# Clustered attention with routed experts: products with v in groups of six key tiles, fourteen exp tiles, two small additions on ScalarE

## The chip, the cores and the metric

The kernel runs on one core of a Trainium2 chip. The metric is the device time of one execution in microseconds. The engines are named as in the profile: PE is TensorE's matrix products, PEld its loads of weights, DVE is VectorE, ACT is ScalarE, POOL is GpSimd, SP is SyncE, whose queue issues most DMAs. Each engine works through its own queue in order, and semaphores order the engines among each other.

## The reference

Two stages. The first is an attention over 4 batches x 8 heads x 768 rows of 64 elements in which a query sees only the keys of its own cluster; the second sends each row of the result to one of eight experts, or to none.

```python
q_assign = argmax(q_n @ c_n.T)            # 16 clusters a head; k likewise
mask = q_assign[:, :, :, None] == k_assign[:, :, None, :]
scores = where(mask, scale * (q @ k.T), -1e9)
attn = exp(scores - scores.max(-1))
attn = attn / (attn.sum(-1) + 1e-9)
x = (attn @ v), heads side by side         # 3072 rows x 512
...
do_compute = x @ w_skip > 0                # other rows pass unchanged
e_idx = argmax(xc @ w_gate)                # softmax over 8 experts gives gate_w
y = gate_w * (relu(xc @ w1[e]) @ w2[e])
out[do_compute] = xc + y
```

## The kernel before

The attention works on pairs of heads: 4 batches x 4 pairs are 16 pairs, numbered 0 to 15. A pair has 24 score steps (`score`, line 596): two halves of 384 queries (`hf`), six key tiles of 128 (`kt`), two heads (`a`). One step is two matrix products into one PSUM bank (lines 602 and 603), the exp on ScalarE into a tile of the ring `PT` (line 605), and an addition on GpSimd into the running sum of the half (lines 611 and 617). The scores stand transposed, with keys on the partitions, so the exp tiles are the right-hand side of the products with v.

Those products are `avs` (line 619). A call takes some key tiles of one half and issues, for each tile and head, one product into PSUM bank 7, the heads in the upper and the lower 64 partitions (128x64 tiles of the array, where the scores use 128x128). In the records each product shows as two. With `GROUP = 3`, a pair has four calls of six products, each set to wait for the last exp that it reads. The ring has `NPT = 12` tiles of 384 + 1 columns; exp number n goes to tile n mod 12.

Everything else of the stage runs between the steps of other pairs: for the next pair the row maxima (`smax`, line 562: one product, line 567, and one reduce on VectorE, line 569, 24 a pair) and the rows that carry them into the scores (`mneg`, `mrows`, lines 576 to 589); for the pair after that the products with the centroids (`sims`), the choice of the cluster (`assign` and `first_max`, five VectorE operations, lines 492 to 505), the split into a rounded part on ScalarE and a rest on VectorE (`split_hi` line 419, `split_lo` line 429) and the mask rows (`masks`); for the pair before, the sums (`sums` line 664, `recip` line 681), and the scaled output (`xout`: transposes, line 727, and six scaled copies on ScalarE, line 749). After every fourth pair the routing of a batch (`route_gates`, `route_slots`) is spread over the next pairs in small VectorE operations, among them lines 495, 912, 915 and 987.

The order of all this is written out by hand. `PLAN` gives each piece a due time in score steps, relative to its own pair; `FIRST` replaces some for the first pairs; `steps` puts all pieces of all pairs into one heap and emits them by due time. A piece that is a generator gives a number and comes back that many steps later. So one program order results, and each engine keeps to its part of it. The calls of `avs` come 1.6 steps behind their last tile: at 7.6, 13.6, 19.6 and 25.6 (which is 1.6 of the next pair). At 7.5 to 7.68 of a pair stand also `recip`, `xout`, `split_hi` and the last three operations of `assign`; at 19.65 to 19.7 a `split_lo`, the copies of `mrows` and operations of the routing.

Seven PSUM banks serve all but `avs`: `take` draws the bank that was given back first, and `give` puts it back behind the others, in program order.

`early_lists` gathers, near the end of pair 14, the first rows that an expert gets, and computes their gates in `slot_gates` (lines 1199 to 1204) from three columns. `group_hidden` and `group_result` serve rows beyond an expert's 256 places.

Of the kernel before, what the change touches and what calls it, by code (L numbers as in the profile page):

```python
# [13 lines left out]
F32 = mybir.dt.float32  # L14
# [4 lines left out]
AF = mybir.ActivationFunctionType  # L19
# [4 lines left out]
P = 128  # L24
H, S, D, NCL = 8, 768, 64, 16
HP = H // 2
HALF = S // 2
NB = HALF // P
KT = S // P
# [7 lines left out]
E, DM, FF = 8, H * D, 1024  # L37
KD, KF = DM // P, FF // P
CAP = 256
CT = CAP // P  # L40
OT = 64
# [22 lines left out]
    1: {  # L64
        "sims": -42.2, "hi": (-42.4, -42.3), "lo": (-40.1, -40.0), "copies": (-20.9, -20.8, -20.7), "load_v": -14.0,
        "assign": (-36.83, 12.93, 0.2, 0.2, 0.2, 0.2), "masks": (-21.6, 0.1), "smax": (-16.3, 0.95, -0.1),
        "mneg": (-5.3, 5.9), "mrows": ((-4.5, 0.2, 0.05), (6.4, 0.1, 0.05)),
    },
    2: {
        "load": -62.0, "load_v": -37.0, "hi": (-34.25, -28.3), "lo": (-28.35, -22.35), "copies": (-23.3, -23.2, -22.2),  # L70
        "assign": (-34.6, 0.25, 0.02, 6.0, 0.02, 0.02), "masks": (-26.0, 0.12), "smax": (-17.6, 0.97, 0.0), "mneg": (-6.4, 5.2),
    },
}

GROUP = 3


class Kernel:
# [6 lines left out]
    def run(self):  # L85
        tc = self.tc
        with ExitStack() as ctx:
            self.const = ctx.enter_context(tc.tile_pool(name="const", bufs=1))
            self.raw = ctx.enter_context(tc.tile_pool(name="rawp", bufs=RING))
            self.halves = {}  # L90

            self.both = ctx.enter_context(tc.tile_pool(name="both", bufs=1))
            self.D = self.both.tile([P, 66 * 256], F32R, name="D")
            self.NPT = 12
            self.PT = self.const.tile([P, self.NPT, HALF + 1], F32, name="PT")
            with ExitStack() as actx:
                self.attention(actx)
            with ExitStack() as mctx:
                self.experts(mctx)
# [146 lines left out]
    def buffers(self):  # L246

        D, both, last = self.D, self.both, self.nbatch * HP - 1
        assert last % 2 == 1 and last % 3 == 0
        part = lambda at, n, w: [D[:, at + w * j:at + w * (j + 1)] for j in range(n)]  # L250
        ops = [part(at, 4, S) for at in (13824, 0, 3072)]
        self.QM, self.KB = [o[:2] for o in ops], [o[2:] for o in ops]
        self.HI = part(6144, 2, S)
        self.QC = [part(at, 4, S) for at in (7680, 10752)]
        raw = both.tile([P, 2, 2, S], F32, name="raw", tag="raw")
        self.RAW = [raw[:, n] for n in range(2)]
        vt = both.tile([P, 2, KT, P], F32, name="vt", tag="vt")
        self.VT = [self.fix.tile([P, KT, P], F32, name="vt0"), vt[:, 0], vt[:, 1]]
        self.OT = [self.fix.tile([P, S], F32, name=f"oT{n}") for n in range(5)]

        w = part(0, 3, 1024) + [None] * 3 + [D[:, 6144:7168], D[:, 3072:4096]]
        w += part(4096, 2, 1024) + [D[:, 7168:8192], None] + part(8192, 2, 1024) + part(10752, 2, 1024)
        self.W = {"w1h": w[:4], "w1l": w[4:8], "w2h": w[8:12], "w2l": w[12:]}
        self.HT = [u.rearrange("p (f t) -> p f t", t=P) for u in part(13824, 2, 1024)]
        self.X1 = [u.rearrange("p (k t) -> p k t", t=P) for u in part(15872, 2, DM)]
        t = self.PT.rearrange("p n q -> p (n q)")
        self.HS, self.YE, self.XG0 = t[:, :FF], t[:, FF:FF + DM], t[:, FF + DM:FF + 2 * DM]
        self.XO = t[:OT, FF + 2 * DM:FF + 3 * DM]

    def keep_busy(self, n, w=4):  # L270

# [53 lines left out]
    def tasks(self, i):  # L325

        p, last = {**PLAN, **FIRST.get(i, {})}, i == self.npair - 1
        r = [(s, lambda s=s: self.score(i, s)) for s in range(NS)]
        add = lambda t, f, *a: r.append((t, lambda: f(i, *a)))
        if i:  # L330
            add(p["load"], self.load)
        add(p["load_v"], self.load_v)
        if i in (1, 2):
            add(-15.0 - i * NS, self.zero_rows)
        add(p["sims"], self.sims)
        add(p["assign"][0], self.assign, *p["assign"][1:])
        if i:
            for t in range(2):
                add(p["hi"][t], self.split_hi, t)
                add(p["lo"][t], self.split_lo, t)  # L340
            add(p["copies"][0], self.copies_hi)
            for t in range(2):
                add(p["copies"][1 + t], self.copies_lo, t)
            add(p["masks"][0], self.masks, *p["masks"][1:])
        else:
            for n in range(4):
                add(p["hi"][n], self.hi_first, n % 2, n // 2)
                add(p["lo"][n], self.lo_first, n % 2, n // 2)
            add(p["masks"], self.masks_first)
        t0, dt, gap, dt2 = (*p["smax"], p["smax"][1])[:4]  # L350
        for n in range(24):
            add(t0 + dt * n if n < 12 else t0 + 12 * dt + gap + dt2 * (n - 12), self.smax, n)
        for hf in range(2):
            add(p["mneg"][hf], self.mneg, hf)
            add(p["mrows"][hf][0], self.mrows, hf, *p["mrows"][hf][1:])
            for g in range(0, KT, GROUP):
                add(12 * hf + 2 * (g + GROUP) + p["av"], self.avs, hf, range(g, g + GROUP))
        if not last:
            add(p["sums"], self.sums, (0, 1))
            add(p["recip"], self.recip)  # L360
            for hf in range(2):
                add(p["xout"][2 if hf and i == self.npair - 2 else hf], self.xout, hf)
        if i == self.npair - HP - 1:
            for t, f in zip(p["early"], (self.early_lists, self.early_rows)):
                add(t, f)
        if last:
            for t, f, *a in self.ending(i):
                add(t, f, *a)
        elif i % HP == HP - 1:
            add(p["route"][0], self.route_a, i // HP)  # L370
            add(p["route"][1], self.route_gates, i // HP)
            add(p["route"][2], self.route_slots, i // HP)
        return r
# [284 lines left out]
    def sums(self, i, hfs):  # L658

        c, nc = self.st[i], self.nc  # L660
        sp = self.take("sums", [P, HALF])
        w = P // (2 * len(hfs))
        for n, (hf, a) in enumerate((hf, a) for hf in hfs for a in range(2)):
            nc.tensor.matmul(sp[n * w:(n + 1) * w, :], lhsT=self.ones[:, :w], rhs=c[f"acc{hf}{a}"],
                             start=True, stop=True)
        c["sr"] = self.small.tile([P, HALF], F32, name="sr")
        nc.scalar.activation(out=c["sr"], in_=sp, func=AF.Copy, bias=GUARD)
        self.give("sums")
        c["hfs"] = hfs
# [30 lines left out]
    def logits_last(self, i, hf, wait):  # L700
        nc = self.nc
        nc.tensor.matmul(self.last[64:96, :], lhsT=self.wg[:, HP - 1, :],
                         rhs=self.st[i]["oT"][:, hf * HALF:(hf + 1) * HALF], start=True, stop=True)
        yield wait
        self.sl = self.small.tile([P, HALF], F32, name="sr")
        if hf:
            nc.scalar.activation(out=self.sl[:96, :], in_=self.last[:96, :], func=AF.Identity, bias=self.guard[:96, :])
        else:
            nc.vector.tensor_scalar(out=self.sl[:96, :], in0=self.last[:96, :], scalar1=self.guard[:96, :], scalar2=None,
                                    op0=ALU.add)  # L710
        self.give("last")
# [487 lines left out]
    def slot_gates(self, acc, pool, rows, n, tag):  # L1199
        nc = self.nc  # L1200
        g = pool.tile([rows, n], F32, name=f"gate{tag}")
        nc.vector.tensor_tensor(out=g, in0=acc[:, 3, :], in1=acc[:, 4, :], op=ALU.add)
        nc.vector.tensor_tensor(out=g, in0=acc[:, 2, :], in1=g, op=ALU.add)
        return g
# [56 lines left out]
    def experts(self, ctx):  # L1261
# [79 lines left out]
        def group_hidden(w1):  # L1341
# [6 lines left out]
            for k in range(KD):  # L1348
                for c in range(2):
                    nc.tensor.matmul(ph[c * OT:(c + 1) * OT, :], lhsT=xt[:, k, :],  # L1350
                                     rhs=w1[k][:, c * FF // 2:(c + 1) * FF // 2],
                                     start=(k == 0), stop=(k == KD - 1), skip_group_check=True)
            hs = ot.tile([P, KF // 2, P], F32, name="ohs")
            nc.scalar.activation(out=hs.rearrange("p m f -> p (m f)"), in_=ph, func=AF.Relu)
            th = ps_y.tile([P, KF // 2, P], F32, name="py")
            for m in range(KF // 2):
                nc.tensor.transpose(out=th[:, m, :], in_=hs[:, m, :], identity=self.ident)
            ht = ot.tile([P, KF // 2, 2, OT], F32, name="oht2")
            nc.scalar.activation(out=ht.rearrange("p m c t -> p m (c t)"), in_=th, func=AF.Copy)
            return ht  # L1360

        def group_result(ht, w2, oid, og):
            py = ps_y.tile([P, DM // 2], F32, name="py")
            for f in range(KF):
                for c in range(2):
                    nc.tensor.matmul(py[c * OT:(c + 1) * OT, :], lhsT=ht[:, f % (KF // 2), f // (KF // 2), :],
                                     rhs=w2[f // 2][:, f % 2 * DM + c * DM // 2:f % 2 * DM + (c + 1) * DM // 2],
                                     start=(f == 0), stop=(f == KF - 1), skip_group_check=True)
            yo = ot.tile([OT, DM], F32, name="oyo")
            for c in range(2):  # L1370
                cs = slice(c * DM // 2, (c + 1) * DM // 2)
                nc.vector.scalar_tensor_tensor(out=yo[:, cs], in0=py[c * OT:(c + 1) * OT, :], scalar=og, in1=xo[:, cs],
# [118 lines left out]
```

## Time and profile before

| | |
|---|---|
| median of 3 runs | 668.26 us (664.48 to 669.05) |
| the profiled execution | 669.92 us |
| its span, first to last instruction | 668.1 us |
| mean granted TensorE clock | 0.989 |
| PE, DVE, ACT, POOL busy, share of the span | 96%, 76%, 63%, 53% |
| instructions | 12396 |

A row of the timeline gives the start, the duration, the engine, the line, the operation, what it writes and reads, the shapes, how many such instructions were merged, and in brackets the idle time of the engine before it with what ended it. A row of the windows gives the stretch, its length, then for PE, PEld, DVE, ACT and POOL the busy time and the count, then the granted clock, the share of the DMA engines and their rate. A row of a group gives the line, the engine, the shapes and count, then the busy time in us and the mean of one in ns.

### The profile page before, as it was taken

The numbers are of one execution on the slowest core, as the hardware profiler recorded it, in microseconds if no ns is written. First come the engines' busy times: TensorE is split into PE (matmuls) and PEld (weight loads), VectorE is DVE, ScalarE is ACT, GpSimd is POOL, SyncE is SP. The second block draws the span as 40 slices with busy tenths as digits, with TensorE's granted clock in tenths as the row PEclk, the third lists the DMA queues.
The fourth block names the chain that finished last, engine by engine and source line by source line (L and its number), as shares of the span: only waits on it lengthen the run. The fifth ranks groups of instructions, "written<-read, shape, count | busy, mean of one in ns | idle before, by whom it ended". The sixth has DMA issues, their size and how long they took to land.

```text
span 668.1 us, 12396 instructions
## 1 busy us (share of the span) xinstructions
PE 644.7 (96%) x3973; PEld 476.9 (71%) x3973; DVE 505.4 (76%) x1031; ACT 418.3 (63%) x933; POOL 357.3 (53%) x384
## 2 busy tenths in 40 slices
PE   7899999999999999999999998999899999999994
PEld 3666676677766767766767766556699899899793
DVE  7878786698998779997869899685769666765621
ACT  7567677777777777777777776543554544645420
POOL 8876776767767857767767688232032122121101
PEclk9999999999999999999999999799999999999998
DMA  7388557857775666466556541241476666764700
GB/s 213 112 195 230 141 163 205 209 164 189 213 217 139 167 170 161 120 170 173 153 134 167 144 117 59 61 146 64 140 259 219 217 225 234 226 208 166 263 10 34
DMA packets 54355, 110.18 MB, mean 165 GB/s; under 512 B 8615, under 2 KB 22823, under 8 KB 54288
## 3 DMA queue, kind: packets, MB, share of 16 engines
q1 hardware_dynamic: 51232, 101.92, 53.3%
q0 software_dynamic: 2656, 7.24, 3.2%
q8 instruction: 33, 0.54, 0.3%
q14 instruction: 34, 0.28, 0.1%
q10 hardware_dynamic: 400, 0.20, 0.1%
HBM read 61.00 MB, written 10.62 MB: 107 GB/s over the span
## 4 chain that ended last, share of the span: by engine, by line
PE 71%; DMA 10%; issue 9%; DVE 9%; POOL 0%; ACT 0%; POOLq 0%; DVEq 0%
PE ps L628 19%; PE ps L602 10%; PE ps L567 10%; PE ps L603 9%; DMA out<-yo,idw 6%; DVE M L569 3%; PE ps L727 2%; DMA xg<-out,idr 2%; PE ph L1028 2%; PE ph L1027 2%; PE ph L1026 2%; PE ps L584 2%; PE ps L478 1%; PE py L1028 1%; PE py L1026 1%
## 5 line engine op out<-in xcount | busy, mean ns | idle before, releaser
L617 POOL TENSOR_TENSOR acc<-acc,PT 128x384 f32<-128x384 f32 x246 | 240.6, 1006 | 56.8 <-ACT PT L605 56.6
L605 ACT ACTIVATE PT<-ps 128x384 f32<-128x384 f32 x384 | 184.5, 492 | 95.4 <-PE ps L603 78.4
L569 DVE TENSOR_REDUCE M<-ps 128x1 f32<-128x384 f32 x384 | 200.2, 554 | 46.1 <-PE ps L567 45.1
L628 PE MATMUL ps<-PT,vt 128*64 128x385 f32 x768 | 140.2, 500 | 0.0
L602 PE MATMUL ps<-D 98*128 98x384 f32 x384 | 135.1, 352 | 4.3 <-DVE M L569 3.8
L567 PE MATMUL ps<-D 96*128 96x384 f32 x384 | 134.9, 358 | 0.9 <-ACT D L547 0.7
L603 PE MATMUL ps<-D 128*128 128x384 f32 x384 | 130.4, 340 | 0.0
L602 PEld LDWEIGHTS ps<-D 98*128 98x128 f32 x384 | 73.1, 190 | 25.3 <-issue 19.1
L628 PEld LDWEIGHTS ps<-PT,vt 128*64 128x64 f32 x768 | 49.8, 137 | 57.8 <-issue 53.1
L611 POOL TENSOR_TENSOR acc<-PT 128x384 f32<-128x384 f32 x64 | 54.3, 870 | 68.3 <-ACT PT L605 36.6
L567 PEld LDWEIGHTS ps<-D 96*128 96x128 f32 x384 | 73.0, 191 | 21.3 <-issue 7.2
L1184 POOL DMA_INDIRECT out<-yo,idw x15 | 18.7, 1250 | 122.4 <-DVE yo L1060 111.0
L603 PEld LDWEIGHTS ps<-D 128*128 128x128 f32 x384 | 73.3, 191 | 0.0
L1309 DVE SCALAR_TENSOR_TENSOR hl<-ph,hh 128x256 fp32r<-128x256 f32 x56 | 23.7, 423 | 39.5 <-ACT hh L1308 39.5
L1308 ACT ACTIVATE hh<-ph 128x256 fp32r<-128x256 f32 x56 | 21.5, 383 | 46.8 <-PE ph L1028 45.8
L1280 ACT ACTIVATE D<-wraw 128x1024 fp32r<-128x1024 f32 (+1 forms) x45 | 43.9, 1001 | 7.6 <-PE py L1028 6.7
L1027 PE MATMUL ph<-x2h,D 128*128 128x256 f32 x168 | 47.5, 283 | 0.0
L1026 PE MATMUL ph<-x2l,D 128*128 128x256 f32 x168 | 47.4, 283 | 0.0
L1026 PE MATMUL py<-D,hh 128*128 128x512 f32 x112 | 45.1, 402 | 0.0
L749 ACT ACTIVATE x<-ps,rs 128x64 f32<-128x64 f32 x162 | 36.2, 322 | 10.2 <-DVE rs L681 9.1
L429 DVE TENSOR_TENSOR raw<-raw,D 128x768 fp32r<-128x768 f32 x28 | 39.2, 1401 | 0.0
L1281 DVE TENSOR_TENSOR D<-wraw,D 128x1024 fp32r<-128x1024 f32 (+1 forms) x29 | 34.3, 1185 | 6.2 <-ACT D L1280 5.2
(311 smaller groups left out, 1075.8 us busy)
## 6 DMA issues: line engine op xcount, KB each, us to landing
wraw<-w SPq DMA_DIRECT2D x72, 512.0 KB, 3.8
D<-D SPq DMA_DIRECT2D x124, 192.0 KB, 3.7
raw<-qk SPq DMA_DIRECT2D x16, 768.0 KB, 5.4
D<-raw SPq DMA_DIRECT2D x60, 192.0 KB, 4.1
vt<-v SPq DMA_DIRECT2D x16, 384.0 KB, 4.4
out<-x SPq DMA_DIRECT2D x31, 192.0 KB, 3.1
D<-mk SPq DMA_DIRECT2D x120, 24.0 KB, 1.9
out<-yo,idw POOLq DMA_INDIRECT x15, 3.7
```

What stands on the lines that cost most here:

```text
L429: eng.tensor_tensor(out=lo.bitcast(F32R), in0=lo, in1=c[f"hi{t}"].bitcast(F32), op=ALU.subtract)
L567: nc.tensor.matmul(sm, lhsT=c["qm"][a][0:96, j * P:(j + 1) * P], rhs=c["kb"][a][0:96, hf * HALF:(hf + 1) * HALF], start=True, stop=True)
L569: nc.vector.tensor_reduce(out=c["m"][:, j, a, hf:hf + 1], in_=sm, axis=AX.X, op=ALU.max)
L602: nc.tensor.matmul(ps, lhsT=c["kb"][a][0:98, ks], rhs=c["qm"][a][0:98, sl], start=True, stop=False)
L603: nc.tensor.matmul(ps, lhsT=c["kc"][a][:, ks], rhs=c["qc"][a][:, sl], start=False, stop=True)
L605: nc.scalar.activation(out=pt, in_=ps, func=AF.Exp, scale=D ** -0.5)
L611: nc.gpsimd.tensor_tensor(out=acc, in0=self.pt(i, s - 2)[:, :HALF], in1=pt, op=ALU.add)
L617: (nc.vector if dve else nc.gpsimd).tensor_tensor(out=acc, in0=acc, in1=pt, op=ALU.add)
L628: nc.tensor.matmul(av[a * D:(a + 1) * D, :], lhsT=c["vt"][:, kt, a * D:(a + 1) * D], rhs=self.pt(i, hf * 2 * KT + kt * 2 + a), start=(kt = ...
L1026: mm(ps, lhsT=ah, rhs=bl, start=first, stop=False)
L1027: mm(ps, lhsT=ah, rhs=bh, start=False, stop=False)
L1280: nc.scalar.activation(out=h[:, cs], in_=r[:, cs], func=AF.Copy)
```

## The change

`GROUP` becomes 6 for pairs 0 to 14, so that `avs` is called twice a pair, at 13.6 and 25.6, with twelve products a call; the last pair keeps groups of three. The ring gets 14 tiles. To make room, the tile `sr` has one buffer in place of two, and three tiles of the code for rows beyond 256 lie in the ring's memory. In `slot_gates` the one-column case, which is that of `early_lists`, uses two ScalarE activations with the second column as bias in place of two VectorE additions. Two entries of `FIRST` change: the rows of the maxima for pair 1 come 0.2 steps later, and the transposes of `assign` for pair 3 half a step later.

```diff
 FIRST, pair 1:
-        "mneg": (-5.3, 5.9), "mrows": ((-4.5, 0.2, 0.05), (6.4, 0.1, 0.05)),
+        "mneg": (-5.3, 5.9), "mrows": ((-4.3, 0.2, 0.05), (6.4, 0.1, 0.05)),
...
+    3: {"assign": (-41.95, 0.07, 0.02, 1.5, 0.02, 0.02)},
-GROUP = 3
+GROUP, LAST_GROUP = 6, 3
...
-            self.NPT = 12
+            self.NPT = 14
...
+        self.OHS, self.OHT, self.OYO = (t[:, FF + n * DM:FF + (n + 1) * DM] for n in (3, 4, 5))
...
-            for g in range(0, KT, GROUP):
-                add(12 * hf + 2 * (g + GROUP) + p["av"], self.avs, hf, range(g, g + GROUP))
+            group = LAST_GROUP if last else GROUP
+            for g in range(0, KT, group):
+                add(12 * hf + 2 * (g + group) + p["av"], self.avs, hf, range(g, g + group))
...
-        c["sr"] = self.small.tile([P, HALF], F32, name="sr")
+        c["sr"] = self.small.tile([P, HALF], F32, name="sr", bufs=1)
...
         g = pool.tile([rows, n], F32, name=f"gate{tag}")
+        if n == 1 and rows == P:
+            nc.scalar.activation(out=g, in_=acc[:, 3, :], func=AF.Identity, bias=acc[:, 4, :])
+            nc.scalar.activation(out=g, in_=acc[:, 2, :], func=AF.Identity, bias=g)
+            return g
         nc.vector.tensor_tensor(out=g, in0=acc[:, 3, :], in1=acc[:, 4, :], op=ALU.add)
         nc.vector.tensor_tensor(out=g, in0=acc[:, 2, :], in1=g, op=ALU.add)
...
-            hs = ot.tile([P, KF // 2, P], F32, name="ohs")
+            hs = self.OHS.rearrange("p (m f) -> p m f", f=P)
-            ht = ot.tile([P, KF // 2, 2, OT], F32, name="oht2")
+            ht = self.OHT.rearrange("p (m c t) -> p m c t", c=2, t=OT)
-            yo = ot.tile([OT, DM], F32, name="oyo")
+            yo = self.OYO[:OT, :]
```

More of the change, by code (lines that the diff above doesn't have):

```diff
@@ L704, in logits_last @@
         yield wait
-        self.sl = self.small.tile([P, HALF], F32, name="sr")
+        self.sl = self.small.tile([P, HALF], F32, name="sr", bufs=1)
         if hf:
```

## Prediction

> **What bounds the kernel now.** I read the page's busy shares first, then the windows, then the timeline around the groups of products with v.
>
> ```profile
> PE 644.7 (96%) x3973; PEld 476.9 (71%) x3973; DVE 505.4 (76%) x1031; ACT 418.3 (63%) x933; POOL 357.3 (53%) x384
> 27.40:429.60 402.20, 395.99 (x2444) 276.91 (x2443) 333.80 (x666) 293.84 (x707) 284.64 (x301) 0.99 0.60 162
> ```
>
> The second row is the window that holds all score tiles but the ends: TensorE is busy for 396.0 of 402.2 us, VectorE for 333.8. So the attention stage costs what TensorE's queue costs, and a change is worth the matrix time that it removes less the pauses that it makes. The 6.2 us that are missing are mostly one pause, shown below. The experts behind it (from 430 us) keep their work and only start earlier or later.
>
> **Part 1: two groups fewer a pair.** A pair issues its products with v (line 628) in four groups; pairs 0 to 14 get two. The number of products stays, so only what a group costs at its two ends can go.
>
> ```profile
> 258.83 0.49 PE L727 MATMUL ps<-ident,oT 128*128 128x128 f32 x3
> 259.25 2.16 PE L628 MATMUL ps<-PT,vt 128*64 128x385 f32 x12
> ...
> 261.62 0.34 PE L603 MATMUL ps<-D 128*128 128x384 f32 x1
> ...
> 265.30 0.49 PE L512 MATMUL ps<-ident,ss 128*128 128x128 f32 x3
> ...
> 265.80 0.34 PE L602 MATMUL ps<-D 98*128 98x384 f32 x1
> ...
> 410.67 0.14 PEld L628 LDWEIGHTS ps<-PT,vt 128*64 128x64 f32 x2 [0.18 <-issue]
> 410.99 0.14 PEld L628 LDWEIGHTS ps<-PT,vt 128*64 128x64 f32 x2 [0.18 <-issue]
> ```
>
> From three transposes to the second product behind them it takes 261.62 - 258.83 = 2.79 us with a group between, and 265.80 - 265.30 = 0.50 without: a group costs 2.29. Its twelve records are six steps of 0.32 to 0.325 (410.67 to 410.99), 1.94 us. So its ends cost **0.35 us**, and 15 pairs x 2 groups x 0.35 = **10.5 us** go.
>
> **Part 2: the early gates.** Two additions on one column move from VectorE to ScalarE.
>
> ```profile
> 409.95 7.17 POOL L617 TENSOR_TENSOR acc<-acc,PT 128x384 f32<-128x384 f32 x8
> 409.97 2.16 PE L628 MATMUL ps<-PT,vt 128*64 128x385 f32 x12
> 410.43 6.70 DVE L1202 TENSOR_TENSOR gatee<-slotacc 128x1 f32<-128x1 f32 x1
> ...
> 412.52 0.34 PE L567 MATMUL ps<-D 96*128 96x384 f32 x1
> ...
> 414.11 0.33 PE L567 MATMUL ps<-D 96*128 96x384 f32 x1
> 417.60 1.48 DVE L569 TENSOR_REDUCE M<-ps 128x1 f32<-128x384 f32 x3
> 418.20 0.69 PE L602 MATMUL ps<-D 98*128 98x384 f32 x1 [3.76 <-DVE M L569]
> ...
> 421.06 4.03 PE L628 MATMUL ps<-PT,vt 128*64 128x385 f32 x12
> ```
>
> The first addition took 6.70 us for one element a row; it ended when GpSimd's run of eight additions ended. The maxima (line 569) queue behind it on VectorE, TensorE stands 3.76 us, and then its clock is at half (part 4). Between these two groups lie 11.09 us, in pair 8 (253.44 to 259.25) 5.81: 5.28 us, and from 421.06 to 424.88 half of 3.82 more: **7.2 us** go. On ScalarE the two stand ahead of the row that frees a PSUM bank; at the nearest rows' 0.16 to 0.2 us each I charge 0.4. What is late next on VectorE is the two-input operation of line 987, right behind: at 201.77 (below) it took 0.87 beside GpSimd, which is small. The Trainium skill, "SBUF — State Buffer", section "Who interferes with whom", says that such a pair of engines excludes each other for one instruction. By that rule the addition should have waited 1.0 us, not 6.70, so the trace disagrees; by the rule the saving would be as here, for line 987 would wait once.
>
> **Part 3: what the removed groups covered.** The order of all other work stays. Seven PSUM banks go round in the order in which they are given back, two a score step (one score tile, one maximum tile). The fence above shows what that means: the maximum product at 412.52 was not reduced, and seven takes later, at 414.11 + 0.18 = 414.29, which is 1.77 us on, TensorE stopped; it went on 0.05 us after that reduce (417.60 + 0.55). So VectorE may be 1.77 us late between a product and the end of its reduce, no more. The two groups that go, after step 7.6 (call it A) and after 19.6 (B), stand exactly where VectorE and ScalarE have their long blocks. Even with the group in front, pair 0 shows a stop:
>
> ```profile
> 40.07 2.16 PE L628 MATMUL ps<-PT,vt 128*64 128x385 f32 x12
> 42.16 0.45 PE L567 MATMUL ps<-D 96*128 96x384 f32 x1
> ...
> 44.32 0.44 PE L567 MATMUL ps<-D 96*128 96x384 f32 x1
> ...
> 43.72 1.48 DVE L569 TENSOR_REDUCE M<-ps 128x1 f32<-128x384 f32 x3
> ```
>
> The product at 42.16 is reduced at 43.72; seven takes on, TensorE waits until 44.32.
>
> Place A, pair 8:
>
> ```profile
> 241.04 2.16 PE L628 MATMUL ps<-PT,vt 128*64 128x385 f32 x12
> ...
> 241.53 1.36 DVE L500 TENSOR_TENSOR eqc<-eqc,wts 128x384 f32<-128x384 f32 x1
> ...
> 243.50 0.56 DVE L505 TENSOR_TENSOR oh<-wts,mwc 128x384 bf16<-128x384 f32 x1
> 243.98 1.02 DVE L569 TENSOR_REDUCE M<-ps 128x1 f32<-128x384 f32 x2
> ...
> L500 DVE TENSOR_TENSOR eqc<-eqc,wts 128x384 f32<-128x384 f32 x14 | 12.0, 858 | 0.0
> ```
>
> Without the group the maximum product starts at 240.95, and the one that needs its bank is due at 242.72. Its reduce stands behind the reciprocals and lines 500, 503 and 505 of `assign`, none of which waits for the group (their inputs come from transposes ahead of it); it still starts at 243.98 and ends at 244.53, so TensorE goes on at 244.58: **1.86 us** late. (ScalarE's block, six scaled rows and a `split_hi`, ends at 243.7; its tile is needed 0.35 us after that point, so it adds nothing.) The block is shorter where line 500 meets no GpSimd: 1.36 here, mean (12.0 - 1.21)/13 = 0.83 in pairs 1 to 13, where the first of the 14, at 41.30 in pair 0, took 1.21. So 1.86 - 0.53 = 1.33 on the mean; 13 x 1.33 = 17.3, and for pair 14, which has no `assign` there but a scaling and a routing step, I take 1.0, an estimate from the short blocks: **18.3 us**. Behind the stopped score product stand the next score tiles, so ScalarE's exps, GpSimd's sums and the next maxima all wait for the same time; none of them is due before the next group, which is more than 1.5 us away.
>
> Place B, where a score tile comes first, so that the bank is due 2.12 us after the place:
>
> ```profile
> 173.54 2.16 PE L628 MATMUL ps<-PT,vt 128*64 128x385 f32 x12
> 173.79 1.55 DVE L429 TENSOR_TENSOR raw<-raw,D 128x768 fp32r<-128x768 f32 x1
> 176.14 0.94 DVE L915 TENSOR_TENSOR g<-g,vals 128x6 f32<-128x6 f32 x1
> 176.99 1.01 DVE L569 TENSOR_REDUCE M<-ps 128x1 f32<-128x384 f32 x2
> ...
> 253.44 2.16 PE L628 MATMUL ps<-PT,vt 128*64 128x385 f32 x12
> 255.33 0.64 DVE L495 TENSOR_TENSOR eqe<-L,mxe 128x48 f32<-128x48 f32 x1
> ...
> 201.77 0.87 DVE L987 TENSOR_TENSOR cc<-ohd,ecode 128x48 f32<-128x48 bf16 x1
> ...
> 225.69 2.16 PE L628 MATMUL ps<-PT,vt 128*64 128x385 f32 x12
> 225.94 1.61 DVE L429 TENSOR_TENSOR raw<-raw,D 128x768 fp32r<-128x768 f32 x1
> ```
>
> Pair 5: bank free at 176.99 + 0.60 = 177.59, due at 173.45 + 2.12 = 175.57, 2.0 late; so in 5, 9, 13. Pair 8, by its block's end at 255.97: 1.0; so in 4, 8, 12. In 6 and 10 the 0.87 of line 987 lies behind `split_lo`: 1.4. In 1, 2, 3, 7, 11, `split_lo` alone (225.94 to 227.55): 0.4. Sum 6.0 + 3.1 + 2.8 + 2.0 = 13.9. Pair 0 would be 2.6 late by the fence before, of which 1.1 comes back where it later waits for VectorE anyway (54.17, below): 1.5. **15.4 us.** At the two groups that grow to 4.0 us VectorE's and ScalarE's blocks were covered already, so nothing comes back there.
>
> **Part 4: the clock.**
>
> ```profile
> 418.05:424.88 6.83, 6.68 (x21) 3.67 (x21) 4.84 (x14) 2.87 (x4) 0.00 (x0) 0.50 0.20 47
> 479.49:482.90 3.41, 1.60 (x7) 0.84 (x6) 3.41 (x8) 3.41 (x7) 0.00 (x0) 1.00 0.47 150
> 482.90:486.30 3.40, 3.40 (x13) 2.80 (x12) 3.16 (x6) 1.99 (x5) 0.00 (x0) 0.50 0.93 331
> 52.83:56.24 3.41, 2.32 (x17) 1.83 (x17) 2.56 (x9) 1.87 (x5) 1.53 (x2) 1.00 0.95 243
> 54.17 0.55 PE L584 MATMUL ps<-ident,MX 128*128 128x128 f32 x3 [1.09 <-DVE MX L576]
> ```
>
> A 3.41 us stretch with TensorE busy for 1.60 was followed by 3.40 us at clock 0.50; one with 2.32 was not. Eight of the new stops (1.75 to 2.6 us: A where line 500 is long, in four pairs, and B in 0, 5, 9, 13) leave about 1.5 to 1.7 busy if they fall wholly into one stretch. I take two or three drops at 3.4/2 us: **+4 us**; bounds 0 and 8 x 1.7 = 14. The Trainium skill, "TensorE: Matmul & The Clock Gate", section "Part 1: The HAM clock gate", halves the clock after a whole idle window of some 3.4 us. By that rule these stops cost no clock, and the time would be 685; the row 479.49 speaks against it.
>
> **Small edits.** Two more exp tiles: tile n is overwritten by exp n + 14, whose readers stand ahead on TensorE and GpSimd; with 12, exp 12 and 13 would wait for the group. `sr` in one buffer: written once a pair, read 2.3 steps later. The overflow tiles in PT have no reader in flight. The two moved times of pairs 1 and 3 shift one set of transposes by one step: I take nothing, between 0.5 us either way (the length of such a set, 0.49 above). Without this cover the tiles would cost an exp's wait at each group.
>
> **Sum**: -10.5 - 7.2 + 0.4 + 18.3 + 15.4 + 4 = +20.4. The profiled execution took 669.92 us; 690.3. The median of the runs shown lies 1.66 below it: **689 us**.
>
> **Rivals.**
> (a) *Faster*: the stops don't come. It is decided at A: if the reduce behind `assign` ends within 1.77 us of its product, TensorE never stops. Then 669.9 - 10.5 - 6.8 - 1.7 = 651. For it speaks that TensorE runs full through the stage now; against it 40.07 to 44.32, and that the block's start hangs on nothing that moves. 0.12.
> (b) *The banks carry half*: blocks shorter or sooner by some 0.7 us each, as where GpSimd is idle: stops of 17 us cancel the gains, 668. 0.07.
> (c) *The gates don't bring what they say*: line 987 takes the place of the addition and starves as long: 689 + 7 = 696. Against: 0.87 at 201.77. 0.07.
> (d) *The clock drops at nearly every stop*, 1.1 us ones too: 24 x 1.7 = 41 in place of 4: 726; half of them, 706. The row 52.83 speaks against. 0.08.
> My forecast (stops as read, up to eight drops: 677 to 700): 0.66.
>
> **Numbers.** About 1% (6.7 us) is what a measurement of this kernel can tell from no change. Range 669 to 706: forecast and (c), the upper edge of (b) and the lower part of (d). Faster 0.12, same 0.07, slower 0.81.
>
> **What would show it.** Right: line 628 in 24-record groups of 4.0 us; in each of pairs 1 to 13 a TensorE pause of 1 to 2 us some 1.8 us behind the transposes of line 727 at A, put down to line 569; a shorter one after line 584 at B; GpSimd and ScalarE no busier; line 1202's early row gone from VectorE. Wrong: TensorE at full pace through A, or pauses put down to ScalarE or GpSimd. Should the exp of step 11 not be done at the longer group, a wait for line 605 would stand ahead of line 628.

## The result, and the profile after

The changed kernel takes **699.0 us** (median of 4 runs, 697.73 to 699.78) against 667.55 in the same runs of the kernel before: ratio 1.047, 95% interval 1.0428 to 1.0511. It is slower by 31 us; forecast were 689, range 669 to 706. The profiled execution took 699.78 us, 29.9 more than that of before.

The page of the changed kernel, busy shares and clock in 40 slices:

```profile
PE 653.7 (94%) x3973; PEld 482.0 (69%) x3973; DVE 493.1 (71%) x1029; ACT 407.8 (58%) x935; POOL 363.2 (52%) x384
PEclk9989999999989999999999999999999999999998
```

VectorE's and ScalarE's shares fell, GpSimd's hardly changed, and TensorE's went from 96% to 94% of a longer span: TensorE waits. For whom, says the view of waits (engine, line, releaser: us in total, times, longest), limited to TensorE:

```profile
PE ps L605 <- DVE M L572: 10.3, 12, 1.7
PE ps L528 <- DVE M L572: 2.9, 1, 2.9
PE ps L587 <- DVE MX L579: 2.9, 5, 1.2
PE ps L969 <- DVE M L572: 2.2, 2, 1.3
PE ps L570 <- ACT x L752: 2.2, 6, 0.6
```

Lines have moved by three: 605 is the score product that was 602, 570 the maximum product (567), 572 its reduce (569), 631 the product with v (628). Before, the first of these rows was one wait, the one behind the gates. Now the reduces hold TensorE at a dozen places by the first row alone. A wait is counted here only beyond the time in which the product before it is still drawn as busy, so the rows understate the stops; start to start is the better reading. Place A of pair 8, TensorE and VectorE in the timeline:

```profile
262.77 0.42 PE L570 MATMUL ps<-D 96*128 96x384 f32 x1
...
264.28 0.33 PE L606 MATMUL ps<-D 128*128 128x384 f32 x1
264.92 0.55 PE L817 MATMUL ps<-ident,gs 128*128 128x128 f32 x3 [0.31 <-ACT x L752]
266.50 0.55 PE L817 MATMUL ps<-ident,gs 128*128 128x128 f32 x3 [1.03 <-DVE M L572]
...
268.75 4.10 PE L631 MATMUL ps<-PT,vt 128*64 128x385 f32 x24
272.79 0.44 PE L570 MATMUL ps<-D 96*128 96x384 f32 x1
...
263.44 1.36 DVE L503 TENSOR_TENSOR eqc<-eqc,wts 128x384 f32<-128x384 f32 x1
264.83 0.55 DVE L506 TENSOR_REDUCE mwc<-eqc 128x24 f32<-128x384 f32 x1
265.42 0.56 DVE L508 TENSOR_TENSOR oh<-wts,mwc 128x384 bf16<-128x384 f32 x1
265.89 1.94 DVE L572 TENSOR_REDUCE M<-ps 128x1 f32<-128x384 f32 x4
```

The maximum product of 262.77 is reduced from 265.89 to 266.44, behind the same three operations as before, and 0.06 us later, at 266.50, the product that needs its bank starts. The 0.31 us before it, for ScalarE's scaled rows (line 752), cost nothing of their own: the wait for VectorE ends later. The long group then takes 4.04 us (268.75 to 272.79), the products of two groups with one pair of ends in place of two.

Place B of pair 5, and the clock in the windows (length, busy times and counts of PE, PEld, DVE, ACT, POOL, then the granted clock) around it:

```profile
189.23 0.44 PE L570 MATMUL ps<-D 96*128 96x384 f32 x1
191.34 0.44 PE L605 MATMUL ps<-D 98*128 98x384 f32 x1 [1.67 <-DVE M L572]
...
187.50 1.61 DVE L432 TENSOR_TENSOR raw<-raw,D 128x768 fp32r<-128x768 f32 x1
189.03 0.97 DVE L915 CAST vals<-g 128x6 bf16<-128x6 f32 x1
190.04 0.78 DVE L918 TENSOR_TENSOR g<-g,vals 128x6 f32<-128x6 f32 x1
190.74 1.94 DVE L572 TENSOR_REDUCE M<-ps 128x1 f32<-128x384 f32 x4
...
188.77:192.18 3.41, 1.74 (x9) 1.27 (x9) 3.38 (x7) 1.67 (x5) 3.41 (x4) 1.00 0.49 151
192.18:195.59 3.41, 3.41 (x14) 1.78 (x14) 3.38 (x8) 2.20 (x8) 2.16 (x3) 0.50 1.06 265
```

The stop, 2.11 us from start to start, left 1.74 us busy in a stretch of 3.41, and the next 3.41 us ran at half clock.

### The profile page after: what moved, and what is told of

It reads as the page before. It is cut to its first block, busy times and chain, and to the rows that moved or that the text cites. A ratio compares the mean times of both kernels' runs of the same rounds, so it can differ in the third digit from the quotient of the medians.

```text
span 698.0 us, 12396 instructions
## 1 busy us (share of the span) xinstructions
PE 653.7 (94%) x3973; PEld 482.0 (69%) x3973; DVE 493.1 (71%) x1029; ACT 407.8 (58%) x935; POOL 363.2 (52%) x384
## 4 chain that ended last, share of the span: by engine, by line
PE 57%; DVE 19%; DMA 11%; issue 9%; ACT 1%; SPq 1%; POOL 0%; POOLq 0%; DVEq 0%; ACTq 0%
PE ps L631 18%; DVE M L572 8%; PE ps L605 7%; DMA out<-yo,idw 6%; PE ps L570 6%; PE ps L606 6%; DVE raw L432 2%; DMA xg<-out,idr 2%; PE ps L481 2%; PE ph L1030 2%; PE ph L1029 2%; PE ph L1031 2%; PE ps L587 1%; PE ps L667 1%; DVE eqc L503 1%
## 5 line engine op out<-in xcount | busy, mean ns | idle before, releaser
L620 POOL TENSOR_TENSOR acc<-acc,PT 128x384 f32<-128x384 f32 x246 | 243.7, 1019 | 44.0 <-ACT PT L608 43.8
L572 DVE TENSOR_REDUCE M<-ps 128x1 f32<-128x384 f32 x384 | 195.4, 550 | 90.6 <-PE ps L570 90.1
L608 ACT ACTIVATE PT<-ps 128x384 f32<-128x384 f32 x384 | 175.6, 498 | 133.9 <-PE ps L606 99.5
L605 PE MATMUL ps<-D 98*128 98x384 f32 x384 | 139.9, 364 | 13.4 <-DVE M L572 10.3
L570 PE MATMUL ps<-D 96*128 96x384 f32 x384 | 138.5, 367 | 4.9 <-ACT x L752 2.2
L631 PE MATMUL ps<-PT,vt 128*64 128x385 f32 x768 | 136.5, 504 | 0.0
L606 PE MATMUL ps<-D 128*128 128x384 f32 x384 | 132.4, 345 | 0.0
L614 POOL TENSOR_TENSOR acc<-PT 128x384 f32<-128x384 f32 x64 | 55.7, 890 | 108.5 <-ACT PT L608 66.2
L631 PEld LDWEIGHTS ps<-PT,vt 128*64 128x64 f32 x768 | 53.5, 141 | 66.3 <-issue 63.8
L606 PEld LDWEIGHTS ps<-D 128*128 128x128 f32 x384 | 74.8, 195 | 0.0
```

Of the source, the lines that this page charges most:

```text
L570: nc.tensor.matmul(sm, lhsT=c["qm"][a][0:96, j * P:(j + 1) * P], rhs=c["kb"][a][0:96, hf * HALF:(hf + 1) * HALF], start=True, stop=True)
L572: nc.vector.tensor_reduce(out=c["m"][:, j, a, hf:hf + 1], in_=sm, axis=AX.X, op=ALU.max)
L605: nc.tensor.matmul(ps, lhsT=c["kb"][a][0:98, ks], rhs=c["qm"][a][0:98, sl], start=True, stop=False)
L606: nc.tensor.matmul(ps, lhsT=c["kc"][a][:, ks], rhs=c["qc"][a][:, sl], start=False, stop=True)
L608: nc.scalar.activation(out=pt, in_=ps, func=AF.Exp, scale=D ** -0.5)
L614: nc.gpsimd.tensor_tensor(out=acc, in0=self.pt(i, s - 2)[:, :HALF], in1=pt, op=ALU.add)
```

## Experiments

Theory: the two groups that went had covered VectorE's blocks at A and B, whose reduces free the PSUM banks; the stops let the clock fall. Rivals: the longer group, the 14 tiles or the new order cost by themselves; VectorE is short of time wherever its work stands. The ratios are to the kernel before in the same job (medians 668.2, 668.3 and 667.6 us).

**e1, the gates alone.** The kernel before with the `slot_gates` branch of the change.

> The kernel before with one edit: the two early additions go to ScalarE. My theory of the gates: the 3.76 us pause of TensorE and the half clock behind it go, 7.2 us less 0.4 for ScalarE, so 661 us against 667.6. Rival: the two-input operation of line 987, which moves into the place of the addition, is starved as long by GpSimd's run of eight; then 667.

Measured 667.01 us, ratio 0.9992 (0.9979 to 1.0005): the rival holds. VectorE in the timeline:

```profile
410.43 6.75 DVE L987 TENSOR_TENSOR cc<-ohd,ecode 128x48 f32<-128x48 bf16 x1
417.22 0.20 DVE L990 TENSOR_REDUCE c<-cc 128x6 f32<-128x48 f32 x1
417.34 1.48 DVE L569 TENSOR_REDUCE M<-ps 128x1 f32<-128x384 f32 x3
```

Line 987 took the addition's place and its 6.7 us. It was never a matter of one element.

**e2, the blocks of A moved.** Changed kernel with

```diff
-"assign": (-42.45, 0.07, 0.02, 2.0, 0.02, 0.02)    "masks": (-34.5, 0.12)   "xout": (31.52, ...)
+"assign": (-42.45, 0.07, 0.02, 8.05, 0.02, 0.02)   "masks": (-26.0, 0.12)   "xout": (37.5, ...)
 FIRST, pair 3:
-"assign": (-41.95, 0.07, 0.02, 1.5, 0.02, 0.02)
+"assign": (-41.95, 0.07, 0.02, 7.55, 0.02, 0.02)
```

`xout` of pair 14 keeps its times.

> The changed kernel, with the blocks at place A put beside the long group: the last three VectorE operations of assign go from step 7.64 to 13.69, the first half of xout from 7.52 to 13.5, and the mask rows, which need assign, to step 22. My theory (the removed groups had covered these blocks): the stops at A go. In the trace of the changed kernel steps 8 to 14 of pairs 1 to 14 are 23.5 us longer than before beyond the 1.94 us of the grown group, three half-clock stretches included, so 699 - 23 = 676. Rival 1 (the longer group, the 14 tiles or the order of the exps cost by themselves, wherever the blocks stand): 699. Rival 2 (VectorE as a whole is the bound of the new order): the time shows up at the next place, 690 or more.

675.22 us, ratio 1.0116 (1.0096 to 1.0136): 24 us off by due times alone, as forecast to 1 us. Rivals 1 and 2 fall for A.

**e3, the blocks of B moved.**

```diff
-"lo": (-34.35, -28.35), "copies": (-23.3, -23.2, -23.1)   GATES 43.67, 43.68 / 67.67, 67.68   SLOTS 91.67, 91.68
+"lo": (-34.35, -22.35), "copies": (-23.3, -23.2, -22.2)   GATES 49.64, 49.65 / 73.64, 73.65   SLOTS 97.64, 97.65
 FIRST, pair 2:
-"lo": (-28.35, -22.35), "copies": (-23.3, -23.2, -22.2), "assign": (..., 6.0, ...),  "masks": (-26.0, 0.12)
+"lo": (-22.36, -22.35), "copies": (-23.3, -22.3, -22.2), "assign": (..., 12.0, ...), "masks": (-22.0, 0.12)
```

> The changed kernel, with the blocks at place B put beside the long group: the second split_lo from step 19.65 to 25.65 with the copies behind it, the routing steps of 19.67 to 25.64, and in pair 0 the first split_lo and three operations of assign from 19.65 to 25.65. Theory: the stops at B go, 18 us in steps 20 to 24 of pairs 0 to 13 and some 6 us of half clock in the pairs behind them, so 699 - 24 = 675; 680 if the drops of the clock come from A as well. Rival 1: 699. Rival 2: 690 or more.

680.95 us, ratio 1.0213 (1.0191 to 1.0235): 18 off. Steps 20 to 24 of pairs 2 to 13 are now 0.2 us longer than before the change, where they were up to 2.0. Less than 24 came back for two reasons: pairs 6 and 10 still drop the clock behind A, and a stop in pair 1 is new, the next point.

**e4, both.**

> Both moves together. Theory: no stop of TensorE over 0.5 us is left between pair 1 and 14, and what remains is what parts 1 and 2 of the prediction gave: 667.6 - 10.5 - 6.8 = 650, with up to 4 us for blocks that no longer fit beside one group (VectorE has some 4 to 5 us of work at step 13.6, ScalarE 2.7): 650 to 655, faster than both kernels. Rival 1: near 699. Rival 2: 675 or more, since the same VectorE work is only pressed into fewer places.

664.79 us, ratio 0.9964 (0.9951 to 0.9977): a little ahead of before, yet 10 to 15 us short of what I expected. In pairs 2 to 14 TensorE is nowhere idle for more than 0.6 us. Of what is missing, 5 us (664.79 to 659.8, as e5 shows) stand at one place, of my own making:

```profile
48.78 0.33 PE L607 MATMUL ps<-D 128*128 128x384 f32 x1
52.60 0.50 PE L529 MATMUL ps<-ident_bf,oh 128*128 128x128 bf16 x3 [3.48 <-DVE oh L509]
```

The mask products of pair 2 waited for an `assign` that I had moved too late, with 6.8 us of half clock behind. Most of the rest is that a group that goes is worth less than its 0.35 us, as the pairs of e5 show.

**e5, that `assign` beside the first long group.** In `FIRST`, pair 2: `"assign": (-34.6, 0.25, 0.02, 0.02, 0.02, 0.02), "masks": (-26.0, 0.12)`.

> As both moves together, but the three operations of assign that pair 0 does for pair 2 go beside its first long group (step 13.7) and the mask rows stay at 22. My theory of the 12 us that the two moves still lacked: in pair 0 I had put that assign at 25.7 and the mask products behind it, where TensorE stood 3.5 us (48.78 to 52.60) and ran 6.83 us at half clock after it, 7 us in all. Then 664.8 - 7 = 658, ahead of both kernels by more than 1%. Rival (VectorE is short of time in pairs 0 and 1 in any order): the stop shows up at the next wait for VectorE, 663 to 665.

**659.8 us** (659.23 to 660.82), ratio 0.988 (0.9854 to 0.9906): ahead of both kernels, 2 us above what I expected. Place A of pair 8 now, TensorE and then VectorE:

```profile
242.99 0.49 PE L731 MATMUL ps<-ident,oT 128*128 128x128 f32 x3
243.41 4.10 PE L632 MATMUL ps<-PT,vt 128*64 128x385 f32 x24
247.44 0.44 PE L571 MATMUL ps<-D 96*128 96x384 f32 x1
...
243.75 1.57 DVE L433 TENSOR_TENSOR raw<-raw,D 128x768 fp32r<-128x768 f32 x1
245.25 0.94 DVE L875 TENSOR_REDUCE L<-lp 128x54 f32<-128x432 f32 x1
246.10 0.54 DVE L504 TENSOR_TENSOR eqc<-eqc,wts 128x384 f32<-128x384 f32 x1
247.27 0.56 DVE L509 TENSOR_TENSOR oh<-wts,mwc 128x384 bf16<-128x384 f32 x1
```

Four microseconds of VectorE stand beside the group. What the grouping is then worth is small: an ordinary pair is 0.25 us shorter than before the change, not 2 x 0.35 = 0.70; the rest goes into 0.2 us at B, where TensorE waits for a bank whose exp stands behind the rows of the maxima on ScalarE, and into mask products at a place of their own. The pause behind the early gates is gone here too; e8 below, which keeps groups of three and takes away that pause alone, reaches 661.12. So e5 is 1.3 us ahead of the best that was found without regrouping.

**e6, the stops filled.** Changed kernel with idle bf16 products ahead of the stops.

```diff
+            for t, n in ((10.85, na), (23.95, nb), (21.95, 0 if i else 13)):   # na 5 to 10, nb 0 to 8 by pair
+                if n: r.append((t, lambda n=n: self.keep_busy(n)))
```

> The changed kernel, with idle products (bf16, 128x512, results unused, into the bank of the products with v while it is free) put in TensorE's queue just ahead of its stops: 5 to 10 at A, 5 to 8 at the long stops of B, 13 ahead of the mask products of pair 0, each some 0.22 us. VectorE's order, and so the end of each stop, stays; only the idle time goes. Theory (half the clock's time is lost because TensorE idles in the stops): the half-clock stretches of pairs 0 to 14 (23.9 us in the changed kernel, 12 us lost) go, 699 - 12 + up to 3 for products that last beyond a stop: 687 to 690. Rival (the clock falls for another reason, or the stops are longer because of it): 699 or more.

690.48 us, ratio 1.0332 (1.0296 to 1.0368): half a microsecond above the upper end. From pair 1 on no half clock is left in the attention; the mean granted clock is 0.993 where the changed kernel has 0.978. The pairs are as long as those of the changed kernel less the 12 us of its drops, but for 2.6 us in all, where products last beyond a stop. So at least 8.5 us of the 31 were the clock, and idle time in the stops was its cause.

**e7, groups of three, all else of the change kept** (`GROUP, LAST_GROUP = 3, 3`).

> The changed kernel with groups of three in every pair, everything else of the change kept: 14 tiles, sr in one buffer, the gates on ScalarE, the two moved times. Theory (the grouping alone makes the kernel slower): as the kernel before with the gates alone, 667. Rival (the ring or the moved times cost): 670 or more.

668.79 us, ratio 1.0011 (0.9991 to 1.0032). The ring, `sr` and the moved times cost nothing that can be measured: the grouping alone made the kernel slower.

**e8, the early gather behind the gates**, in the kernel before:

```diff
-        yield 0.2
-        self.gather(self.xe[:, 0, :], rd, self.ntok - S)
         yield (91.66,)
         self.early = wr, self.slot_gates(acc, const, P, 1, "e")
+        yield (91.95,)
+        self.gather(self.xe[:, 0, :], rd, self.ntok - S)
```

> The kernel before, gates on VectorE as there, with the gather of the early rows issued after them (step 19.95 in place of 13.87). On ScalarE's account the gates brought nothing, since line 987 in their place took 6.75 us too. Theory: GpSimd is behind at that place because the gather held its queue for some 2.8 us, and a VectorE operation with two inputs waits as long as GpSimd's additions follow each other without a gap; without the gather in front the addition takes 1 us at most and the pause goes: 667.6 - 7 = 660.5. Rival (something in the operation itself, or in its place behind the maxima): again 6.7 us, 667.

661.12 us (661.0 to 661.33), ratio 0.9897 (0.9863 to 0.9931): the pause is gone, and this is the cheapest gain found. VectorE, then GpSimd:

```profile
410.37 0.59 DVE L1202 TENSOR_TENSOR gatee<-slotacc 128x1 f32<-128x1 f32 x1
411.00 0.79 DVE L1203 TENSOR_TENSOR gatee<-slotacc,gatee 128x1 f32<-128x1 f32 x1
...
409.12 3.65 POOL L617 TENSOR_TENSOR acc<-acc,PT 128x384 f32<-128x384 f32 x4
412.94 1.22 POOL L1179 DMA_INDIRECT xe<-out,idre  x1 [0.17 <-issue]
```

That the early gather's place decides is shown. That it does so through GpSimd's unbroken run is only argued: here too the additions follow each other closely, and VectorE got in at the first change-over.

**e9, the ring at 12 tiles**, on e5.

> As the best version so far (both moves, pair 2's assign early), with 12 exp tiles in place of 14. Exps 12 and 13 of a half then overwrite tiles 0 and 1, which the first four records of the long group read, so they wait until about 0.7 us into that group; ScalarE's scaled rows and split_hi stand behind them. Theory: the group lasts 4.0 us and ScalarE has some 3.6 us to do in it, so the wait stays covered: 660 to 662, and the two tiles are hardly needed. Rival (the prediction's sentence that the tiles would cost an exp's wait at each group, 27 places of about 0.5 us): 670 or more.

671.28 us, ratio 1.0059 (1.0036 to 1.0081), 11.5 over e5. My reasoning had the order the wrong way round: exps 12 and 13 stand ahead of the products in the program, so the exps don't wait for the products; the products wait for the exps, and the first key tile's products read the exps of the next half, so that the output is wrong. This run tells of the order and the time alone. All records of line 632, by who ended their engine's idle time (e5 has 4.0 us, 23 times, in this row):

```profile
  ACT PT L609: 9.6, 50
```

The long group becomes 4.41 us, 0.37 more. Fourteen tiles are what groups of six need, not a cover.

## Why the prediction was right, and where it was off

Sign, mechanism and places came out as read; the range held, with the forecast 10 us too low. By its terms, with steps compared from start to start between the traces of before and after:

- *Ends of groups, 0.35 us each*: the stretches that lost a group are 2.29 us shorter, those that grew 1.94 longer in pairs without a stop. As predicted.
- *A, 18.3 us*: steps 8 to 14 of pairs 1 to 14 are 23.5 us longer beyond the grown group; three drops of the clock among them (5.1) leave 18.4. That the sum agrees to 0.1 is partly luck. Pairs 4 and 12 lost 1.0 where I read 1.9, since line 503 took 0.53 us there and not 1.35. Pairs 6 and 10 lost 1.8 to 1.9 where I read 1.4, since line 964 of the routing took 1.21 and 1.07 us there and not 0.40.
- *B, 15.4 us*: steps 20 to 24 of pairs 0 to 13 add 18.05; less 0.9 that pair 1 regained and 1.3 of half clock, 15.8. Pair by pair 0.3, 0.3, 1.1, 2.0, 1.5, 0.2 for pairs 2 to 7, where 0.4, 0.4, 1.0, 2.0, 1.4, 0.4 were read.
- *The clock, 4 us*: **the term that was off**. Seven stretches at half clock stand behind the stops, 23.9 us (45.40 to 52.23, and from 93.19, 192.18, 209.24, 325.29, 424.28), 12 us lost; e6 gave 8.5 back, net of what its products cost. I had counted two or three drops, asking that a stop of 1.75 us or more fall wholly into one stretch and leave 1.5 to 1.7 us busy. Six stops were followed by a drop (A of pairs 2, 6 and 10, B of 0, 5 and 13), the one in pair 0 by two stretches. The condition was too strict: stretches with 1.73 to 2.08 us busy were followed by half clock too.
- *The gates, 7.2 us*: right in size by luck, wrong in cause. The time went (pair 14 and the first steps of 15 lost 6.5), but e1 shows that the edit brought none of it; rival (c) was true of the edit. In e7, with the gates on ScalarE too, line 990 took 7.01 us. In the changed kernel the place comes later, and the same line takes 0.20 us, although another run of GpSimd's additions is on its way:

```profile
448.40 0.20 DVE L990 TENSOR_TENSOR cc<-ohd,ecode 128x48 f32<-128x48 bf16 x1
447.66 4.44 POOL L620 TENSOR_TENSOR acc<-acc,PT 128x384 f32<-128x384 f32 x5
```

  The first of these additions lasts 0.86 us, to 448.52, so line 990 got in at a change-over; why it did here and not in e1 is open. The two operations on ScalarE took 0.30 and 0.29 us, where 0.4 was charged, and TensorE does not wait for them.
- *Small edits*: nothing, as e7 shows. The sentence that 12 tiles would cost an exp's wait was wrong in its mechanism (e9).

The sum by the measured terms is -10.5 - 6.5 + 18.4 + 15.8 + 12 + 1.7 for one more drop in pair 0 (from 21.51) = +30.9; measured in the profiled execution, +29.9. That drop is not the grouping's: e7 has it, and e2 to e5 don't. The sum leaves out 1.1 us that pair 0 lost at A, which I had put at nothing, 0.9 that pairs 6 and 10 regained just ahead of A, and the 1.7 of the drop at 482.90, which the changed kernel doesn't have; with these it is +29.4.

## What to carry to other kernels

A long run of one engine's work is also the cover for the other engines' blocks beside it: before merging two runs, list what stands beside the one that goes, and move it along. With a ring of banks the allowance is plain arithmetic (seven takes, 1.77 us), and it can be read from any stall of the old trace. A slow instruction that waits for another engine need not be mended by moving that instruction: in e1 the next of its kind took its place.

## What the runs showed of the hardware

In this trace TensorE's clock changes on a fixed grid of 3.41 us (from the drop at 45.40 to that at 93.19 are 14 stretches, to 192.18 another 29), and it goes with the busy time in the stretch before, not with a whole idle stretch. Stretches of the changed kernel's grid, the first four followed by half clock, the last two not:

```profile
41.99:45.40 3.41, 1.46 (x9) 1.15 (x7) 3.34 (x4) 2.64 (x6) 3.41 (x4) 1.00 1.05 225
205.83:209.24 3.41, 1.80 (x14) 1.32 (x13) 3.38 (x7) 2.69 (x8) 2.11 (x3) 1.00 0.20 44
321.88:325.29 3.41, 1.86 (x15) 1.51 (x14) 3.38 (x7) 2.94 (x9) 1.75 (x3) 1.00 0.27 56
89.78:93.19 3.41, 2.08 (x11) 1.51 (x10) 3.34 (x8) 2.90 (x10) 1.53 (x3) 1.00 0.01 2
...
263.85:267.26 3.41, 2.07 (x14) 1.52 (x13) 3.34 (x6) 2.89 (x9) 1.67 (x3) 1.00 0.17 39
304.82:308.23 3.41, 2.15 (x11) 1.57 (x10) 3.38 (x5) 2.76 (x7) 3.41 (x4) 1.00 0.34 75
```

In this trace the border lies near 2.1 us of 3.41, and it is not sharp in the busy time as drawn: 2.08 was followed by half clock, 2.07 was not, and in e5 a stretch with 1.81 (17.27 to 20.69) was not either. The Trainium skill, "TensorE: Matmul & The Clock Gate", section "Part 1: The HAM clock gate", names an idle window of some 3.4 us as what brings the lower clock. In these rows no stretch was idle throughout, so they differ, and the measurement decides.

A VectorE operation with two inputs in SBUF took 6.75 us in e1, until a run of eight GpSimd additions ended, and in e5 line 991 took 2.30 us (412.11), also to the end of such a run (414.34). It took 0.59 us at the same place in e8 and 0.20 us in the changed kernel (448.40), where it got in at the first change-over. The Trainium skill, "SBUF — State Buffer", section "Who interferes with whom", has such a pair of engines exclude each other for one instruction. e8 and the changed kernel agree, e1 and e5 do not, and what decides at a change-over stays open.
